# Two V rows per matmul, identity weights loaded once per twelve matmuls, and half of wd loaded in 16 pieces

## The chip, the cores and the metric

One core of one Trainium2 chip. The metric is the device time of one execution in microseconds (us). Runs agree within about 0.2%. Kernels are compared only within the same rounds.

## The reference, cut to what matters

```python
# B=4 sequences, one new token, D=640, 32 heads of Dh=192, 4096 cached positions, F=1536; bf16
h  = x + attention(layernorm(x) @ wq, k_cache, v_cache) @ wo
h2 = h + (silu(layernorm(h) @ w_gate) * (layernorm(h) @ w_up)) @ w_down
```

K and V are 201 MB each. Everything else is small: wq and wo 7.9 MB each, w_gate, w_up and w_down (wg, wu, wd below) 2.0 MB each. All of it is read once, 424 MB in all.

## The kernel before

K and V come in 128 loads of 3 MB (the last V in two halves) into a ring of six slots. A load is issued when its slot's last reader is done. For each of 64 steps (a pair of heads and a sequence), VectorE multiplies K by the query in two halves, TensorE sums groups of 16 products by an identity matmul, VectorE finishes the sums and the maximum, ScalarE takes the exponent, and TensorE multiplies the probabilities by V:

```python
def red(i, h):                      # 12 matmuls with the same weights, 128 times
    for j in range(J):              # J = 12
        matmul(psR[n % 3][:, 0:512], lhsT=identH, rhs=prod[n % NPR][:, :, j*16:(j+1)*16],
               start=(j == 0), stop=(j == J - 1))

def pv(i, lo=0, hi=T):              # 64 matmuls of 192 columns, 64 times
    for t in range(lo, hi):
        n = t % 4
        matmul(psO[p % 2][32*n:32*n + 8, 0:192], lhsT=pbuf[b][:, t, :], rhs=v[:, t, :], ...)

def o_t(p):                         # folds the four rows of psO, transposed; 16 times
    for j in range(3):
        for hh in range(2):
            matmul(psO[...], lhsT=orow[p % 2][:, j::3], rhs=r32[:, hh:8:2])
```

At the end wg, wu and wd are loaded into three slots of the ring, in that order, each by one transfer of 128 partitions; wd is waited for as a whole:

```python
wd_land = dma("sp", ... wdsb[:, :, :] <- wd viewed as "(q c) n -> q (c n)", c=12, [behind(n0 + 2)])
...
for c in range(12):
    for n in range(4):
        matmul(psH[32*n:32*n + 4, 0:160], lhsT=guT[:, c, 0:4], rhs=wdsb[:, c, n*160:(n+1)*160])  # waits: guT, wd_land
```

## Time and profile before

| | before |
|---|---|
| time, median of the first three runs | 1005.88 us |
| TensorE matmul busy, weight-load busy | 645.7, 296.7 us |
| TensorE instructions, matmuls and weight loads | 6736 + 6736 |
| load queue busy, share of 16 DMA engines | 98.9% |
| instruction packets (queue 8) | 53 |

The page of the kernel before: part 1 (busy time and share of each engine), the DMA row of part 2 (tenths busy in 40 slices), part 3 (queue: packets, MB, share of 16 engines) and the start of part 4 (the chain of waits by engine):

```profile
PE 645.7 (64%) x6736; PEld 296.7 (30%) x6736; DVE 547.5 (55%) x450; ACT 119.7 (12%) x412; POOL 4.5 (0%) x19
...
DMA  9999999999999999999999999999999999999995
...
q1 hardware_dynamic: 21472, 424.29, 98.9%
q8 instruction: 53, 0.87, 0.4%
...
DMA 68%; PE 21%; DVE 10%; SPq 1%; issue 0%; ACTq 0%; ACT 0%
```

No compute engine is near its limit, and the DMA engines are busy to the end. The line easily passed over is queue 8. Its 53 packets are 16 KB each (16384 bytes in the trace). Over TensorE's stream of 6736 + 6736 instructions that is 64.5 bytes and 254 instructions a packet, so I take them for the fetches of this stream.

The trace has 16 landing times for each of these loads, which I take for the shares of the 16 DMA engines of the page (by my count of the packet records, 16.1 packets are in flight on average between 100 and 900 us). This is my own listing of them for wd, the last load (us from the span's start):

```
988.47 988.71 988.81 988.91 989.19 990.08 991.86 993.05 | 998.10 998.36 998.43 999.02 999.31 999.55 999.75 999.92
```

Eight engines (below, the early eight) finish some 9 us ahead of the other eight (the late ones). The gap between the means of the two halves is 0.45 us for the first load of the run, 4.5 us at 504 us, and 9.0 us for wg. A load counts as landed only with its sixteenth part (wd's came at 999.92 us, and the wd matmuls that waited for it started at 1000.05), so the late eight set the pace.

The timeline of the last 16 us (start us, us taken, engine, line, operation, tiles; in brackets the engine's idle time before and what ended it), lnT being the normalized input of the second half and guT the input of the wd matmuls:

```profile
988.89 0.70 PE L398 MATMUL pb<-r,orow 128*64 128x4 f32 x12 [0.43 <-ACT orow L387]
...
993.25 0.35 DVE L256 STREAM_TRANSPOSE lnT<-lnrow 128x160 bf16<-128x160 bf16 x1
...
995.38 0.10 PEld L502 LDWEIGHTS pb<-wu_sb,lnT 128*4 128x4 bf16 x8 [0.67 <-DMA wu_sb<-in_B_w_up_dram]
...
997.87 0.85 DVE L508 STREAM_TRANSPOSE guT<-gu 128x384 bf16<-128x384 bf16 x1
...
1000.05 1.77 PE L512 MATMUL pb<-wd_sb,guT 128*4 128x160 bf16 x48 [2.90 <-DMA wd_sb<-in_B_w_down_dram]
```

guT is ready at 998.72 us, but the wd matmuls start at 1000.05, when wd's last part has landed (999.92).

### The profile page before, as it was taken

Reading aid. Unit: us, or ns where it says so; the run is one execution under the profiler, and the core shown is the slowest. Engines: PE = TensorE matmul, PEld = TensorE weight load, DVE = VectorE, ACT = ScalarE, POOL = GpSimd, SP = SyncE. Lnnn points to the kernel's source line nnn. Section 1 sums busy time; section 2 is a strip of 40 time slices with the busy share of each in tenths; the row PEclk is TensorE's granted clock in tenths of the full one; section 3 lists DMA queues with packets and bytes.
Section 4 is the critical chain, followed back from the end, with each engine's and each line's share of the span. In section 5 each row is a group of like instructions: output and inputs, shape, how many; then the busy total and the mean of one; then the engine's idle time right before and its main releaser. Section 6 shows DMA issues by size and latency. Waiting matters only on the chain.

```text
span 1004.3 us, 14803 instructions
## 1 busy us (share of the span) xinstructions
PE 645.7 (64%) x6736; PEld 296.7 (30%) x6736; DVE 547.5 (55%) x450; ACT 119.7 (12%) x412; POOL 4.5 (0%) x19
## 2 busy tenths in 40 slices
PE   0676666666576576576576676676676676576585
PEld 0232232333232232232232232232332332232243
DVE  2546546546546546546546546546546546546562
ACT  0111011011011011011010110110111010111012
POOL 1000000000000000000000000000000000000000
PEclk9787887887887888887887887887887877877887
DMA  9999999999999999999999999999999999999995
GB/s 394 426 435 430 426 431 427 428 431 427 429 429 427 429 429 431 428 427 431 427 430 428 430 426 431 425 433 430 425 431 429 428 429 428 431 428 429 428 425 248
DMA packets 21582, 425.24 MB, mean 423 GB/s; under 512 B 2448, under 2 KB 2448, under 8 KB 4496
## 3 DMA queue, kind: packets, MB, share of 16 engines
q1 hardware_dynamic: 21472, 424.29, 98.9%
q8 instruction: 53, 0.87, 0.4%
q14 instruction: 9, 0.07, 0.0%
q10 hardware_dynamic: 48, 0.01, 0.0%
HBM read 424.29 MB, written 0.01 MB: 422 GB/s over the span
## 4 chain that ended last, share of the span: by engine, by line
DMA 68%; PE 21%; DVE 10%; SPq 1%; issue 0%; ACTq 0%; ACT 0%
DMA ring<-in_A_k_cache_dram 64%; PE pb L319 15%; DVE prod L309 7%; PE pb L381 3%; DMA wd_sb<-in_B_w_down_dram 2%; DMA xrow<-in_A_x_dram 2%; DVE sc L325 1%; PE pb L334 1%; SPq L294 1%; PE pb L276 1%; DVE msb L330 0%; PE pb L344 0%; PE pb L365 0%; PE pb L398 0%; SPq L300 0%
## 5 line engine op out<-in xcount | busy, mean ns | idle before, releaser
L309 DVE TENSOR_TENSOR prod<-ring,qb 128x6144 f16<-128x6144 bf16 x128 | 429.2, 3354 | 308.3 <-DMA ring<-in_A_k_cache_dram 301.2
L319 PE MATMUL pb<-prod,identH 128*128 128x512 f16 x1536 | 470.6, 472 | 3.2 <-DVE prod L309 3.2
L319 PEld LDWEIGHTS pb<-prod,identH 128*128 128x128 f16 x1536 | 167.8, 116 | 262.1 <-issue 168.9
L334 PE MATMUL pb<-identF,msb 128*1 128x128 f32 x128 | 34.7, 369 | 320.5 <-DVE msb L330 320.5
L325 DVE TENSOR_REDUCE sc<-pb 128x32 f32<-128x512 f32 x128 | 88.0, 688 | 111.8 <-PE pb L319 111.8
L334 PEld LDWEIGHTS pb<-identF,msb 128*1 128x1 f32 x128 | 5.5, 80 | 335.9 <-DVE msb L330 335.9
L349 ACT ACTIVATE negM<-pb 128x1 f32<-128x1 f32 x64 | 11.0, 171 | 721.0 <-PE pb L344 721.0
L381 PE MATMUL pb<-ring,pbuf 128*8 128x192 bf16 x4096 | 95.8, 246 | 0.2 <-ACT pbuf L356 0.2
L381 PEld LDWEIGHTS pb<-ring,pbuf 128*8 128x8 bf16 x4096 | 81.3, 87 | 3.7 <-issue 0.4
L356 ACT ACTIVATE pbuf<-sc,negM 64x64 bf16<-64x64 f32 x128 | 73.7, 576 | 3.1
L356 ACT ACTIVATION_READ_ACCUMULATOR pbuf<-sc,negM 64x1 f32 x128 | 41.6, 325 | 0.0
L371 ACT ACTIVATE qb<-pb 128x192 bf16<-128x192 f32 x64 | 21.1, 330 | 102.5 <-PE pb L365 102.5
L344 PEld LDWEIGHTS pb<-negMc,ones_row 1*64 1x64 f32 x256 | 12.8, 136 | 35.0 <-issue 33.4
L344 PE MATMUL pb<-negMc,ones_row 1*64 1x1 f32 x256 | 18.3, 206 | 0.7 <-DVE negMc L338 0.7
L365 PE MATMUL pb<-qsb,sel 4*64 4x192 bf16 x128 | 17.2, 265 | 1.0 <-ACT qsb L280 0.6
L338 DVE TENSOR_REDUCE negMc<-pb 1x2 f32<-1x128 f32 x64 | 17.4, 271 | 0.5 <-PE pb L334 0.5
L246 PE MATMUL pb<-mv,quadm 128*128 128x2 f32 x4 | 1.0, 312 | 23.4 <-DVE mv L244 23.4
L330 DVE TENSOR_REDUCE msb<-sc 128x1 f32<-128x64 f32 x64 | 14.1, 220 | 2.2
L365 PEld LDWEIGHTS pb<-qsb,sel 4*64 4x64 bf16 x128 | 6.7, 101 | 27.9 <-issue 26.3
L398 PE MATMUL pb<-r,orow 128*64 128x4 f32 x192 | 11.1, 233 | 0.4 <-ACT orow L387 0.4
L398 PEld LDWEIGHTS pb<-r,orow 128*64 128x64 f32 x192 | 9.7, 173 | 2.1 <-ACT orow L387 0.7
L242 DVE BATCH_NORM_STATS2 stats<-xrow 128x6 f32<-128x160 bf16 x1 | 0.3, 328 | 16.2 <-DMA xrow<-in_A_x_dram 16.2
(60 smaller groups left out, 71.8 us busy)
## 6 DMA issues: line engine op xcount, KB each, us to landing
ring<-in_A_k_cache_dram SPq DMA_DIRECT2D x64, 3072.0 KB, 30.4
ring<-in_A_v_cache_dram SPq DMA_DIRECT2D x63, 3072.0 KB, 23.4
wq_sb<-in_A_wq_dram SPq DMA_DIRECT2D x1, 7680.0 KB, 21.2
wo<-in_A_wo_dram SPq DMA_DIRECT2D x16, 480.0 KB, 23.8
ring<-in_A_v_cache_dram SPq DMA_DIRECT2D x2, 1536.0 KB, 19.7
wg_sb<-in_B_w_gate_dram SPq DMA_DIRECT2D x1, 1920.0 KB, 26.2
wu_sb<-in_B_w_up_dram SPq DMA_DIRECT2D x1, 1920.0 KB, 19.4
wd_sb<-in_B_w_down_dram SPq DMA_DIRECT2D x1, 1920.0 KB, 23.6
```

The source lines that it names most:

```text
L309: tk["tt", n] = op("dve", lambda e: e.tensor_tensor(out=prod[n % NPR][:, :, :], in0=ring[slot[c]][:, h * TH:(h + 1) * TH, :], in1=qbs[i % ...
L319: tk["red", n] = op("pe", lambda e, j=j: e.matmul(psR[n % 3][:, 0:TH * R], lhsT=identH[:, :], rhs=prod[n % NPR][:, :, j * R:(j + 1) * R], ...
L325: tk["rsum", n] = op("dve", lambda e: e.tensor_reduce(sc[i % 3][:, h * TH:(h + 1) * TH], psR[n % 3][:, 0:TH * R].rearrange("q (t r) -> q t ...
L330: tk["rmax", i] = op("dve", lambda e: e.tensor_reduce(msb[i % 2][:, 0:1], sc[i % 3][:, :], AX.X, ALU.max), [g("rsum", 2 * i), g("rsum", 2 ...
L334: tk["maxT", i] = op("pe", lambda e: e.matmul(psS[0:1, 0:128], lhsT=msb[i % 2][:, 0:1], rhs=identF[:, :], start=True, stop=True), [g("rmax ...
L338: tk["hmax", i] = op("dve", lambda e: e.tensor_reduce(negMc[i % 2][0:1, 0:2], psS[0:1, 0:128].rearrange("o (h q) -> o h q", h=2), AX.X, AL ...
L344: tk["maxB", i] = op("pe", lambda e, hh=hh: e.matmul(psS[64 * hh:64 * hh + 64, 128:129], lhsT=ones_row[0:1, :], rhs=negMc[i % 2][0:1, hh:h ...
L356: tk["exp", i] = op("act", lambda e, hh=hh, r=r: e.activation(out=pbuf[b][r, :, 2 * b + hh], in_=sc[i % 3][r, :], func=ACTF.Exp, bias=negM ...
L365: tk["qb", i] = op("pe", lambda e, hh=hh: e.matmul(psQ[64 * hh:64 * hh + 64, 0:DH], lhsT=sel[32 * n:32 * n + B, b, :], rhs=qsb[32 * n:32 * ...
L371: tk["qbc", i] = op("act", lambda e: e.activation(out=qbs[i % 2][:, :], in_=psQ[:, 0:DH], func=ACTF.Copy, scale=QS), [g("qb", i), g("tt", ...
L381: tk["pv", i] = op("pe", lambda e, t=t, n=n: e.matmul(psO[p % 2][32 * n:32 * n + 2 * B, 0:DH], lhsT=pbuf[b][:, t, :], rhs=v[:, t, :], star ...
L398: tk["oT", p] = op("pe", lambda e, j=j, hh=hh: e.matmul(psO[p % 2][64 * hh:64 * hh + 64, 256 + 4 * j:260 + 4 * j], lhsT=orow[p % 2][:, j:: ...
```

## The change

Its intent: less work and fewer instructions on TensorE, and a better split of the last load over DMA engines. Two V rows go into one matmul (16 stationary columns, 384 moving columns; the two off-diagonal blocks are ignored). The identity weights stay in the array for eleven of twelve matmuls. The two matmuls that spread the maximum become one, and the fold `o_t` needs two accumulating matmuls in place of one. Half of wd (six of twelve rows of each partition) comes in 16 loads of 8 partitions, which are meant for the eight DMA engines that finish early. The other half comes in two loads over all 16.

```diff
+def held_matmul(e, out, lhsT, rhs, start, stop):
+    return e.add_instruction(mybir.InstMatmult(... ldweights=False, ...))
...
-            tk["red", n] = op("pe", lambda e, j=j: e.matmul(
+            tk["red", n] = op("pe", lambda e, j=j: (e.matmul if j == 0 else partial(held_matmul, e))(
...
-        for t in range(lo, hi):
-            n = t % 4
+        for t in range(lo, hi, 2):
+            n = (t // 2) % 4
...
-                psO[p % 2][32 * n:32 * n + 2 * B, 0:DH], lhsT=pbuf[b][:, t, :], rhs=v[:, t, :],
+                psO[p % 2][32 * n:32 * n + 4 * B, 0:2 * DH],
+                lhsT=pbuf[b][:, t:t + 2, :].rearrange("q t m -> q (t m)"),
+                rhs=v[:, t:t + 2, :].rearrange("q t d -> q (t d)"),
...
+                for k in range(2):          # o_t: twice the matmuls
...
-    wd_land = dma("sp", lambda e: e.dma_start(wdsb[:, :, :].rearrange("q c n -> q (c n)"),
-                                              wd[:, :].rearrange("(q c) n -> q (c n)", c=CF)),
-                  S_ring[(n0 + 2) % NS], [behind(n0 + 2)])
+    WDC = [(0, 6, sem("s_wd0")), (6, 10, sem("s_wd1")), (10, CF, sem("s_wd2"))]
+    wd_land = {}
+    for lo, hi, k in WDC:
+        nr = 8 if lo == 0 else 128
+        for r in range(0, 128, nr):
+            t = dma("sp", lambda e, lo=lo, hi=hi, r=r, nr=nr: e.dma_start(
+                wdsb[r:r + nr, lo:hi, :], wd[:, :].rearrange("(q c) n -> q c n", c=CF)[r:r + nr, lo:hi, :]),
+                k, [behind(n0 + 2)])
+        for c in range(lo, hi):
+            wd_land[c] = t
```

More of the change, by code (lines that the diff above doesn't have):

```diff
@@ L1 @@
 import math
+from functools import partial
 import concourse.bass as bass
@@ L91, in emit @@
         block.sync(run("sp"))
+def held_matmul(e, out, lhsT, rhs, start, stop):
+    return e.add_instruction(mybir.InstMatmult(
+        name=e.bass.get_next_instruction_name(), engine=mybir.EngineType.PE, start_tensor_calc=start,
+        stop_tensor_calc=stop, tile_size=(128, 128), tile_position=(0, 0), ldweights=False,
+        ins=[e.lower_ap(rhs), e.lower_ap(lhsT, for_matmul_weights=True)], outs=[e.lower_ap(out)]))
 class ExitGuard:
@@ L118, in build_kernel @@
     NS, NPR = 6, 3
+    OC = 2 * DH
     QS = 2.0 ** -4
@@ L145, in build_kernel @@
     r32 = sb("r32", [128, 32], FP32)
-    ones_row = sb("ones_row", [1, 64], FP32)
+    ones_row = sb("ones_row", [1, 128], FP32)
     epsv = sb("epsv", [128, 1], FP32)
@@ L155, in build_kernel @@
     negMc = [sb(f"negMc{j}", [1, 2], FP32) for j in range(2)]
-    negM = [sb(f"negM{j}", [128, 1], FP32) for j in range(2)]
+    negM = [sb(f"negM{j}", [128, 2], FP32) for j in range(2)]
     lsb = [sb(f"lsb{j}", [128, B], FP32) for j in range(2)]
     invL = sb("invL", [128, B], FP32)
-    orow = [sb(f"orow{j}", [128, DH], FP32) for j in range(2)]
+    orow = [sb(f"orow{j}", [128, 2 * DH], FP32) for j in range(2)]
     OT = [sb(f"OT{j}", [128, 3, B], BF16) for j in range(2)]
@@ L342, in max_b @@
     def max_b(i):
-        for hh in range(2):
-            tk["maxB", i] = op("pe", lambda e, hh=hh: e.matmul(
-                psS[64 * hh:64 * hh + 64, 128:129], lhsT=ones_row[0:1, :], rhs=negMc[i % 2][0:1, hh:hh + 1],
-                start=True, stop=True), [g("hmax", i), pool_done])
+        tk["maxB", i] = op("pe", lambda e: e.matmul(
+            psS[:, 128:130], lhsT=ones_row[0:1, :], rhs=negMc[i % 2][0:1, 0:2],
+            start=True, stop=True), [g("hmax", i), pool_done])
     def neg_m(i):
-        tk["negM", i] = op("act", lambda e: e.activation(out=negM[i % 2][:, :], in_=psS[:, 128:129], func=ACTF.Copy,
+        tk["negM", i] = op("act", lambda e: e.activation(out=negM[i % 2][:, :], in_=psS[:, 128:130], func=ACTF.Copy,
                                                          scale=alpha), [g("maxB", i)])
@@ L356, in exps @@
             tk["exp", i] = op("act", lambda e, hh=hh, r=r: e.activation(
-                out=pbuf[b][r, :, 2 * b + hh], in_=sc[i % 3][r, :], func=ACTF.Exp, bias=negM[i % 2][r, 0:1],
+                out=pbuf[b][r, :, 2 * b + hh], in_=sc[i % 3][r, :], func=ACTF.Exp, bias=negM[i % 2][r, hh:hh + 1],
                 scale=alpha, accum_out=lsb[p % 2][r, b:b + 1]),
@@ L377, in pv @@
         v = ring[slot[c]]
-        for t in range(lo, hi):
-            n = t % 4
+        for t in range(lo, hi, 2):
+            n = (t // 2) % 4
             land = landed[c][min(t // TH, len(landed[c]) - 1)]
             tk["pv", i] = op("pe", lambda e, t=t, n=n: e.matmul(
-                psO[p % 2][32 * n:32 * n + 2 * B, 0:DH], lhsT=pbuf[b][:, t, :], rhs=v[:, t, :],
-                start=(b == 0 and t < 4), stop=(b == B - 1 and t >= T - 4)), [land, g("exp", i), g("otc", p - 2)])
+                psO[p % 2][32 * n:32 * n + 4 * B, 0:2 * DH],
+                lhsT=pbuf[b][:, t:t + 2, :].rearrange("q t m -> q (t m)"),
+                rhs=v[:, t:t + 2, :].rearrange("q t d -> q (t d)"),
+                start=(b == 0 and t < 8), stop=(b == B - 1 and t >= T - 8)), [land, g("exp", i), g("otc", p - 2)])
         released[c] = tk["pv", i]
     def evac(p):
-        tk["evac", p] = op("act", lambda e: e.activation(out=orow[p % 2][:, :], in_=psO[p % 2][:, 0:DH],
+        tk["evac", p] = op("act", lambda e: e.activation(out=orow[p % 2][:, :], in_=psO[p % 2][:, 0:2 * DH],
                                                          func=ACTF.Copy), [g("pv", B * p + B - 1), g("oT", p - 2)])
@@ L397, in o_t @@
             for hh in range(2):
-                tk["oT", p] = op("pe", lambda e, j=j, hh=hh: e.matmul(
-                    psO[p % 2][64 * hh:64 * hh + 64, 256 + 4 * j:260 + 4 * j], lhsT=orow[p % 2][:, j::3],
-                    rhs=r32[:, hh:2 * B:2], start=True, stop=True), [g("evac", p), pool_done])
+                for k in range(2):
+                    tk["oT", p] = op("pe", lambda e, j=j, hh=hh, k=k: e.matmul(
+                        psO[p % 2][64 * hh:64 * hh + 64, OC + B * j:OC + B * (j + 1)],
+                        lhsT=orow[p % 2][:, k * DH + j:(k + 1) * DH:3],
+                        rhs=r32[:, 2 * B * k + hh:2 * B * (k + 1):2], start=(k == 0), stop=(k == 1)),
+                        [g("evac", p), pool_done])
     def inv_l(p):
@@ L406, in o_tc @@
         tk["otc", p] = op("dve", lambda e: e.tensor_tensor(
-            out=OT[p % 2][:, :, :], in0=psO[p % 2][:, 256:256 + 3 * B].rearrange("q (j b) -> q j b", b=B),
+            out=OT[p % 2][:, :, :], in0=psO[p % 2][:, OC:OC + 3 * B].rearrange("q (j b) -> q j b", b=B),
             in1=invL[:, None, :].broadcast_to([128, 3, B]), op=ALU.mult),
@@ L513, in build_kernel @@
                 psH[32 * n:32 * n + B, 0:DQ], lhsT=guT[:, c, 0:B], rhs=wdsb[:, c, n * DQ:(n + 1) * DQ],
-                start=False, stop=(c == CF - 1), skip_group_check=True), [gut, wd_land, ln2])
+                start=False, stop=(c == CF - 1), skip_group_check=True), [gut, wd_land[c], ln2])
     a = op("dve", lambda e: e.tensor_copy(out=outsb[:, :], in_=psH[:, 0:DQ]), [a])
```

## The prediction

> **What bounds it now.** The DMA engines. Page part 3: the load queue is busy 98.9% of 16 engines' span; slices read 9 throughout. TensorE (64%), VectorE (55%) and ScalarE (12%) are not limits; in the chain of waits the ring loads take 64%. Less TensorE work as such buys nothing before the last 30 us.
>
> **What is uneven.** The trace's landing records (16 increments a load, one an engine) split the engines into two groups of eight. For wd, eight land at 988.5 to 993.1 us, eight at 998.1 to 999.9. The gap of the group means grows evenly: 0.45 us at 22 us, 4.5 at 504, 9.2 at the end. Packets run back to back on both, so the late group does extra work: queue 8, "instruction", 53 packets of 16 KB. Their durations repeat with period eight, so I take them to go round eight engines. 53 x 256 = 13568 instructions, TensorE's stream (6736 + 6736). [...] Here a chunk with a fetch lands about 1.4 us late on one engine; 8.7 us x 8 / 53 gives 1.3 us a fetch. Every ring slot waits for the late group, which sets the pace.
>
> **What the change does.**
> 1. PV: 4096 to 2048 matmul and weight-load pairs. Reduction: 1536 weight loads to 128. maxB halves, oT doubles (192 to 384). TensorE's instructions fall from 13472 to about 8100: about 32 fetches, 21 fewer: 21 x 1.3 / 8 = 3.4 us earlier on the late group, hence in all landings; the gap at the end becomes about 5.7 us. This is the main gain; saved matmul time is hidden (at the low clock a reduction matmul takes 427 ns with or without a weight load).
> 2. wd: [...] At the measured 26.8 GB/s an engine (122.9 KB between the wu and wd landings, 4.58 us), the late group ends 2.3 us sooner and the early one 2.3 us later: both about 992 to 996. [...]
> 3. Tail (timeline): the compute from the last K landing to lnT at 993.6 moves with the loads (-3.4), plus oT 24 instead of 12 instructions (+0.6, from 0.70 us now) and a wider evacuation (+0.15). wu is then no longer the wait. guT ends near 996 instead of 998.7, and the wd matmuls start there instead of 1000.05, when wd landed; of the gain wd's landing allows 1.3 us.
>
> **Prediction.** 1005.9 - 3.4 (fetches) - 1.3 (wd) + 0.7 (oT, evacuation) gives 1001.9; [...] 1002.2 us, 8 in 10 within 1000.5 to 1004.6. Faster by over 2%: 0.01; within: 0.98; slower: 0.01.
>
> **What would show it.** Queue 8: about 32 packets. Gap of the landing groups before wd: 5 to 6 us. Busy PE and PEld down much, span down 0.4%. Half wd landed before guT ends. oT about 1.3 us at the tail.
>
> **What would make it wrong.** [...] Fetches whose cost doesn't follow their number. [...] half wd lands after 998. TensorE's clock staying low, so that its 14.6 us period is filled. The 16 extra issues (about 0.4 us each) coming too late.

The sum as it stands comes to 1001.9 us; the forecast is 1002.2. The 0.3 us between them stood for a possible loss through the 8-partition loads, which I guessed at 0 to 2 us; that term is cut, its ground not being shown. Cut too is the assumption that the half of wd in the 16 loads (0.98 MB) would go to the early eight engines; the 2.3 us each way and the 1.3 us for wd rest on it.

The figures of the prediction in the traces: 254 instructions a packet in the kernel before (the prediction counts 256). The packets of queue 8 take 1015 to 1107 ns, the first and last apart, in an order that repeats with every eighth (1072, 1068, 1059, 1099, 1099, 1087, 1018, 1018, then 1074, 1078, 1060, 1107, 1107, 1087, 1018, 1026). A packet of queue 8 began at 239.9 us; between the load whose last part landed at 240.85 us and the next, one landing of the sixteen slipped 1.5 us against the rest. From one reduction matmul's start to the next it is 427 ns (median) at a granted clock of 0.5 and 216 ns at 1.0, in the kernel before and in the changed one, where eleven of twelve have no weight load. One of the 64 steps takes 14.8 us (median). A load's issue took 0.33 or 0.43 us in the kernel before, and the 16 extra ones came 0.34 us apart.

## More of the kernel before

The stretches of the tail (us; busy time and instructions of each engine; then granted TensorE clock, DMA share, GB/s) show DMA share and throughput fall together, as engines finish:

```profile
984.00:989.00 5.00, 4.04 (x139) 3.10 (x140) 0.46 (x2) 3.15 (x8) 0.00 (x0) 1.00 0.94 397
989.00:994.00 5.00, 1.69 (x34) 1.13 (x38) 2.85 (x11) 1.58 (x2) 0.00 (x0) 0.80 0.58 243
```

## The result

1006.42 us, median of four runs (1006.26 to 1006.79), beside 1006.11 us before. The ratio is 1.0003, with a 95% interval of 0.9986 to 1.0021. Ratios here are the mean time of one kernel's runs over that of the other's of the same rounds, so not quite the ratio of the medians that I quote. The change gained nothing; 1002.2 us was forecast, 1000.5 at the least and 1004.6 at the most.

The page after: TensorE's weight loads and instructions and the queues are as forecast. Its matmul busy time is not: it rose from 645.7 to 658.7 us, where the prediction had "Busy PE and PEld down much". The V part raised it (662.2 us in pv_only, 647.5 in held_only, both below); how little such time counts, pad_time shows.

```profile
PE 658.7 (66%) x4752; PEld 121.5 (12%) x3344; DVE 547.6 (55%) x450; ACT 122.6 (12%) x412; POOL 4.5 (0%) x19
...
q1 hardware_dynamic: 21872, 424.29, 99.2%
q8 instruction: 32, 0.52, 0.2%
```

The timeline of the tail after, the same steps as before:

```profile
985.62 1.25 PE L412 MATMUL pb<-r,orow 128*64 128x4 f32 x24 [0.59 <-ACT orow L399]
...
990.73 0.35 DVE L266 STREAM_TRANSPOSE lnT<-lnrow 128x160 bf16<-128x160 bf16 x1
...
994.40 0.10 PEld L526 LDWEIGHTS pb<-wu_sb,lnT 128*4 128x4 bf16 x8 [2.21 <-DMA wu_sb<-in_B_w_up_dram]
...
996.89 0.85 DVE L532 STREAM_TRANSPOSE guT<-gu 128x384 bf16<-128x384 bf16 x1
...
999.39 0.97 PE L536 MATMUL pb<-wd_sb,guT 128*4 128x160 bf16 x24 [3.21 <-DMA wd_sb<-in_B_w_down_dram]
1000.79 1.22 PE L536 MATMUL pb<-wd_sb,guT 128*4 128x160 bf16 x24 [0.43 <-DMA wd_sb<-in_B_w_down_dram]
```

Read it from the top. The fold and lnT come 3.3 and 2.5 us earlier than before, although the fold takes 0.55 us longer: up to here the gain is there. Then TensorE waits 2.21 us for wu, where it had waited 0.67, and 3.21 us for the first half of wd. wu's last part lands at 994.36 us, 1.0 us before its old time although the loads ahead of it land over 3 us before theirs (wg: 987.44 in place of 990.78). wd's last part lands at 1001.53, 1.6 us after its old time.

The stretches of the tail after:

```profile
984.00:989.00 5.00, 3.01 (x56) 2.17 (x56) 1.69 (x7) 0.97 (x3) 0.00 (x0) 0.86 0.97 271
989.00:994.00 5.00, 2.00 (x22) 0.66 (x21) 1.34 (x5) 2.07 (x3) 0.00 (x0) 0.50 0.85 241
```

From 984 to 989 us the DMA share rose (0.94 to 0.97) and the throughput fell from 397 to 271 GB/s. The engines were as busy as before and moved less, so their packets took longer: by my count those of 15360 B that started in this stretch took 851 ns in the median, against 576 before.

So the theory after the result: the fetches were real and gave their gain, and the 8-partition loads took it back, because of the partitions of SBUF that they write while other loads still land. No trace shows by what way one load would hold up another, so the runs test only what can be measured: the same loads over neighbouring partitions or over partitions four apart (wd_step4), and on partitions 0 to 63 or 64 to 127 (wd_low, wd_high). Rivals: the fetches never mattered; the TensorE parts cost what wd gained; many small loads are slow by their size, their reads or their issue.

### The profile page after: what moved, and what is told of

Same layout as the page of the kernel before. It is cut to its first block, busy times and chain, and to the rows that moved or that the text cites. A ratio compares the mean times of both kernels' runs of the same rounds, so it can differ in the third digit from the quotient of the medians.

```text
span 1004.5 us, 9444 instructions
## 1 busy us (share of the span) xinstructions
PE 658.7 (66%) x4752; PEld 121.5 (12%) x3344; DVE 547.6 (55%) x450; ACT 122.6 (12%) x412; POOL 4.5 (0%) x19
## 3 DMA queue, kind: packets, MB, share of 16 engines
q1 hardware_dynamic: 21872, 424.29, 99.2%
## 4 chain that ended last, share of the span: by engine, by line
DMA 67%; PE 21%; DVE 10%; SPq 1%; issue 0%; ACTq 0%; ACT 0%
DMA ring<-in_A_k_cache_dram 63%; PE pb L97 13%; DVE prod L319 7%; PE pb L391 3%; DMA wd_sb<-in_B_w_down_dram 2%; DMA xrow<-in_A_x_dram 2%; PE pb L329 2%; DVE sc L335 1%; PE pb L344 1%; SPq L304 1%; PE pb L353 1%; PE pb L412 1%; PE pb L286 1%; DVE msb L340 1%; SPq L513 0%
## 5 line engine op out<-in xcount | busy, mean ns | idle before, releaser
L319 DVE TENSOR_TENSOR prod<-ring,qb 128x6144 f16<-128x6144 bf16 x128 | 429.1, 3353 | 305.6 <-DMA ring<-in_A_k_cache_dram 299.1
L97 PE MATMUL pb<-prod,identH 128*128 128x512 f16 x1408 | 432.3, 470 | 0.0
L358 ACT ACTIVATE negM<-pb 128x2 f32<-128x2 f32 x64 | 11.0, 172 | 715.6 <-PE pb L353 715.6
L391 PE MATMUL pb<-ring,pbuf 128*16 128x384 bf16 x2048 | 94.7, 326 | 0.2 <-ACT pbuf L365 0.2
L329 PE MATMUL pb<-prod,identH 128*128 128x512 f16 x128 | 61.2, 478 | 3.2 <-DVE prod L319 3.2
L353 PEld LDWEIGHTS pb<-negMc,ones_row 1*128 1x128 f32 x128 | 19.4, 189 | 279.4 <-issue 249.6
L391 PEld LDWEIGHTS pb<-ring,pbuf 128*16 128x16 bf16 x2048 | 46.3, 89 | 27.5 <-issue 0.5
L353 PE MATMUL pb<-negMc,ones_row 1*128 1x2 f32 x128 | 24.9, 262 | 0.7 <-DVE negMc L348 0.7
L412 PE MATMUL pb<-r,orow 128*64 128x4 f32 x384 | 20.0, 231 | 0.6 <-ACT orow L399 0.6
L412 PEld LDWEIGHTS pb<-r,orow 128*64 128x64 f32 x384 | 18.6, 174 | 2.4 <-ACT orow L399 1.0
L329 PEld LDWEIGHTS pb<-prod,identH 128*128 128x128 f16 x128 | 12.6, 99 | 32.1 <-issue 23.7
```

The source lines that it names most:

```text
L97: return e.add_instruction(mybir.InstMatmult(name=e.bass.get_next_instruction_name(), engine=mybir.EngineType.PE, start_tensor_calc=start, ...
L319: tk["tt", n] = op("dve", lambda e: e.tensor_tensor(out=prod[n % NPR][:, :, :], in0=ring[slot[c]][:, h * TH:(h + 1) * TH, :], in1=qbs[i % ...
L329: tk["red", n] = op("pe", lambda e, j=j: (e.matmul if j == 0 else partial(held_matmul, e))(psR[n % 3][:, 0:TH * R], lhsT=identH[:, :], rhs ...
L353: tk["maxB", i] = op("pe", lambda e: e.matmul(psS[:, 128:130], lhsT=ones_row[0:1, :], rhs=negMc[i % 2][0:1, 0:2], start=True, stop=True), ...
L391: tk["pv", i] = op("pe", lambda e, t=t, n=n: e.matmul(psO[p % 2][32 * n:32 * n + 4 * B, 0:2 * DH], lhsT=pbuf[b][:, t:t + 2, :].rearrange(" ...
L412: tk["oT", p] = op("pe", lambda e, j=j, hh=hh, k=k: e.matmul(psO[p % 2][64 * hh:64 * hh + 64, OC + B * j:OC + B * (j + 1)], lhsT=orow[p % ...
```

## The experiments

All but two gave correct results. Packet times below are my own count from the trace's packet records: "7680 B" are the packets of the 16 loads, "15360 B" those of wg, wu (and of an undivided wd), which take 573 to 592 ns undisturbed.

### undo_wd: the change without its wd part

```diff
-    WDC = ...; 16 loads of 8 partitions and 2 of 128
+    wd_land = dma("sp", ... one load of 128 partitions, as before)
```

> The changed kernel with wd loaded again by one transfer of 128 partitions. Theory (fetches are DMA work of the late eight engines[...]): 32 packets on queue 8, gap of the two landing groups 5.2 to 5.8 us at the end, wu lands near 992, wd near 996.5, time 1002.4 us (1001.8 to 1003.2). Rival (instruction fetches cost nothing that is waited for, and the wd part is neutral): 1006.2 us as before.

Measured: 1001.87 us, ratio 0.9952 (0.994 to 0.9965), 32 instruction packets, gap of the landing groups 4.8 us at wg, wu landed at 991.00 and wd at 995.56. The stretch and the step that waited in this run:

```profile
984.00:989.00 5.00, 2.01 (x38) 1.63 (x38) 2.44 (x10) 1.03 (x3) 0.00 (x0) 0.96 0.97 406
...
995.70 1.77 PE L528 MATMUL pb<-wd_sb,guT 128*4 128x160 bf16 x48 [2.83 <-DMA wd_sb<-in_B_w_down_dram]
```

What follows: the TensorE parts gain 4.8 us (0.0048 x 1006), and the wd part takes all of it back. The rival that the TensorE parts cost what wd gained is out. That it is the fetches through which these parts gain is not shown yet; pad43 and pad_time are for that.

### only_wd: the kernel before with the new wd loads alone

```diff
-    wd_land = dma("sp", ... one load of 128 partitions)
+    WDC = ...; 16 loads of 8 partitions and 2 of 128, as in the change
```

> The kernel before with the new wd loads alone. Theory [...]: 53 packets on queue 8; the 7680-byte packets take a median well over their shortest; the wu landing moves later than 995.3 us by 1 to 3 us, wd is complete at 1001 to 1004 us, time 1007 to 1010 us. Rival (the rebalancing of engines works as meant, the loss of the whole change comes from the TensorE parts): wd complete by 998, time 1004.6 us.

Measured: 1010.75 us, ratio 1.0042 (1.0029 to 1.0056). wu landed at 1000.07 (995.34 before), wd at 1005.96. The 7680 B packets took 428 ns in the median and up to 624; their shortest took 291. The stretch:

```profile
984.00:989.00 5.00, 3.99 (x136) 3.05 (x136) 0.68 (x3) 2.98 (x8) 0.00 (x0) 1.00 0.94 255
```

The loss is in the wd loads alone, 4.2 us here. wu came even later than I expected (4.7 us, not 1 to 3), and so did wd and the end.

### wd_step4: the 16 loads over partitions four apart

```diff
-        for r in range(0, 128, nr):          # partitions r .. r+7
+        rows = [slice(32*j + s, 32*j + s + 29, 4) for j in range(4) for s in range(4)]   # 8 partitions, 4 apart
```

> The changed kernel with the same 16 loads of 8 partitions, but of partitions 4 apart[...]. Theory [...]: the first eight loads (partitions 0 to 63) have packets of 291 to 310 ns; those of partitions 64 to 127 [...] are slower; time 1002.5 to 1004.5 us. Rival (the cost is that of many small loads: their number, their size of 7680 bytes, their issue): packets as before (median 398 ns, up to 567) and time 1006.4 us.

Measured: 1006.34 us, ratio 0.9998 (0.9986 to 1.0011). The time missed the expectation; the packets met it. The first 32 packets of 7680 B, those that began before 986.4 us, took 291 to 301 ns; then, as the loads of partitions 64 to 127 began, they rose, to a median of 566 ns between 986.6 and 994 us. Of the 82 packets of 15360 B that started after 984.5 us, 49 took more than 800 ns, up to 1349. Both about doubled, and this hits wu, which TensorE waits for next.

Neighbouring partitions cost something too. In the change itself the first packet of 7680 B began at 983.58 us, so if an engine takes its loads in order, none was at its ninth load (partition 64) before 985.9 (eight packets of 291 ns). Yet the 21 packets of 15360 B that began there from 984.3 to 985.9 took 738 to 1052 ns, against 573 to 581 in wd_step4, which differs only in the partitions of each load. From 985 to 986 us some ten packets of 15360 B were in flight at a time (10.2 on average) and four of 7680 B (3.9). Four writers were there beside ten others, and all ten were slow. How the slowness gets to the others stays open.

Whether the bytes of partitions 64 to 127 or merely the later loads are slow, this run can't tell; wd_low and wd_high can.

### wd_low and wd_high: the same loads, written to one half of the partitions

```diff
+    wdx = spare room behind wd in the same ring slot
+            if nr == 8 and (rs.start < 64) != True:       # wd_high: != False
+                dst, ds = wdx, slice(rs.start - 64, rs.stop - 64, 4)   # wd_high: + 64
```

The sources, sizes, engines and issues are those of wd_step4. The wd matmuls of that half use 64 partitions.

> wd_step4 with the second eight loads writing their bytes to spare room on partitions 0 to 63 in place of 64 to 127; same sources, sizes, engines and issue. The result is wrong on purpose (the first half of wd is used on 64 partitions alone). Theory [...]: the 7680-byte packets take 291 to 310 ns throughout, the late engines' 15360-byte packets of wu 573 to 590 ns, wu lands near 991, wd is complete near 995.5 us, time 1001.5 us (1000.8 to 1002.8). Rival (small loads, their reads from memory or their issue are slow): as wd_step4, 1006.3 us.

Measured: 1002.64 us, ratio 0.9962 (0.9948 to 0.9976). All 128 packets of 7680 B took 291 to 298 ns, and those of 15360 B 573 to 592, but for one of 1065. wu landed at 991.18, wd at 997.78, later than the 995.5 I expected.

> The opposite of wd_low: all 16 loads write to partitions 64 to 127 (wrong result on purpose). Theory: 7680-byte packets at 560 ns or more from the start while late engines still load, the late engines' wu packets near 1000 to 1150 ns from 984 us on, wu lands after 995, time 1008 us or more (1007 to 1013). Rival: as wd_step4, 1006.3 us.

Measured: 1010.37 us, ratio 1.0039 (1.0026 to 1.0053). The 7680 B packets took 565 ns in the median, wu's packets 1126, and wu landed at 997.11. The stretches of wd_step4:

```profile
984.00:989.00 5.00, 3.20 (x56) 2.23 (x56) 1.69 (x7) 0.92 (x3) 0.00 (x0) 0.78 1.01 301
```

of wd_low:

```profile
984.00:989.00 5.00, 3.20 (x59) 2.22 (x56) 1.69 (x7) 1.11 (x3) 0.00 (x0) 0.82 0.97 387
```

and of wd_high:

```profile
984.00:989.00 5.00, 2.87 (x55) 1.95 (x55) 1.79 (x8) 0.81 (x3) 0.00 (x0) 1.00 1.04 237
```

Only the destination differs between the three, and with it how many partitions the matmuls of that half use: 387, 301 and 237 GB/s with none, half and all of the loads on partitions 64 to 127, and 1002.64, 1006.34 and 1010.37 us. The rival of slow small loads falls: in wd_low they take 291 to 298 ns, where 291 is the shortest in the change itself. What counts is which partitions they write while other loads are still landing.

Yet wd_low is no faster than undo_wd, and its wd landed 2.2 us later. Its landings tell why. Each of the 16 loads has eight landings with its data, so eight engines carry them, 16 packets each. Six engines had landed wu by 985.5 us. But from 986 to 987 us only four packets of 7680 B were in flight, and two engines landed their share of wd's second piece at 987.93 and 988.24. Had they carried 16 packets of 291 ns after wu (984.26 at the earliest), and then the 1.6 us of that piece (an estimate: eight packets of 196 ns, the shortest of this size in the changed kernel's trace; 102 ns for the third piece), they would have landed it at 990.5. So at least two of the early eight carried none of the 16 loads, and at least two of the late ones did. The last two shares of wd fit: two late engines landed wu at 990.45 and 990.77; 4.7 us for the 16 packets and 1.6 and 0.8 us for the two other pieces give 997.5 and 997.8, and they landed at 997.45 and 997.78. The half of wd did not go where the time was free. Besides, fewer fetches had already cut the gap of 9.0 us to 4.8, and moving half of wd changes it by about 4.6 (an estimate, twice the 2.3 us of the prediction), so there was little left to balance.

### wd_chunks: three pieces, each over all 16 engines

```diff
-        nr = 8 if lo == 0 else 128
+        nr = 128
```

> The changed kernel with wd in its three pieces, each one load of 128 partitions over 16 engines. Theory: as undo_wd, with the first wd matmuls not later; 1002.0 us (1001.4 to 1003.0), and no 7680-byte packet slowed beyond some 300 ns. Rival (splitting wd into pieces is what costs): 1005 to 1006.5 us.

Measured: 1001.54 us, ratio 0.9949 (0.9935 to 0.9963). Its 7680 B packets took 291 to 302 ns; wu landed at 991.10 and the last of wd at 995.76. The stretch, and the wd matmuls, which no longer wait for wd:

```profile
984.00:989.00 5.00, 3.01 (x56) 2.17 (x56) 1.69 (x7) 0.97 (x3) 0.00 (x0) 0.93 0.97 400
...
996.11 1.00 PE L536 MATMUL pb<-wd_sb,guT 128*4 128x160 bf16 x48 [1.61 <-DVE guT L532]
```

This beats both kernels, by 0.5%. It is not told apart from undo_wd (0.9949 and 0.9952, with intervals that overlap). undo_wd's wait for wd is gone, but guT ended 1.6 us later in this profile (996.05 against 994.43 us), so whether cutting wd in pieces gains anything stays open.

### pad43 and pad_time: instructions back without work, and work without instructions

```diff
             pv(i - 2)
+            for _ in range(43):                       # pad43: 86 instructions a step
+                matmul(psS[0:1, 400:401], lhsT=identB[:, 0:1], rhs=identB[:, 0:1])
+            for d in range(12):                       # pad_time instead: 13 instructions a step
+                (matmul if d == 0 else held_matmul)(psS[:, 260:500], lhsT=identB, rhs=identB, 240 columns)
```

Both start from undo_wd.

> undo_wd with 43 useless one-column matmuls (86 instructions) per batch in 62 of the 64 steps: TensorE's instruction count is that of the kernel before again, with no new load and nothing waiting for them. Theory (instruction fetches delay the late engines): 53 packets on queue 8, gap of the landing groups near 9 us again, time 1005.3 us (1004.6 to 1006.2), 3.4 us over undo_wd. Rival (the gain of undo_wd comes from fewer or quicker TensorE operations, not from fetches): gap 5.4 us, time within 0.5 us of 1001.9.

> Control for pad43: undo_wd with TensorE time added in few instructions, one weight load and 12 matmuls of 240 columns (13 instructions) per step. Theory (fetches): about 35 packets on queue 8, gap below 6.3 us, time 1002.4 us (1001.7 to 1003.2). Rival (TensorE time is what counts): as slow as pad43 or slower, over 1004.5 us.

Measured: pad43 1007.22 us, ratio 1.001 (0.9998 to 1.0023); pad_time 1003.09 us, ratio 0.9969 (0.9956 to 0.9983). Busy times and queue 8 of pad43:

```profile
PE 728.9 (73%) x7418; PEld 195.8 (19%) x6010; DVE 547.7 (54%) x450; ACT 122.5 (12%) x412; POOL 4.5 (0%) x19
...
q8 instruction: 52, 0.85, 0.3%
```

and of pad_time:

```profile
PE 729.6 (73%) x5496; PEld 127.9 (13%) x3406; DVE 547.4 (55%) x450; ACT 122.6 (12%) x412; POOL 4.5 (0%) x19
...
q8 instruction: 35, 0.57, 0.2%
```

The two add the same matmul time, 68 us. With the instructions the gap at wg is 8.9 us again and wg lands at 991.07; with the time alone the gap is 5.5 and wg lands at 987.90. The fetches cause the gap; TensorE's time does not. pad43 is 1.9 us slower than the 1005.3 that I expected, 1.0 over the range. Both run the padding in the last step of the loop too, where TensorE's 1.1 us (68 over 62 steps) is on the chain; that would account for a part of it, though I did not test it apart. In pad43 the wd matmuls wait for guT (1001.84 us), not for wd (1000.22), so the landings are the cleaner measure here.

### held_only and pv_only: the two TensorE parts apart

```diff
 held_only: the kernel before, with held_matmul for j > 0 in red()
 pv_only:   undo_wd, with e.matmul for every j in red()
```

> The kernel before with the held identity weights alone: 1408 weight loads fewer. Theory: 47 or 48 packets on queue 8, gap near 8.2 us, 0.9 us under before (ratio 0.999). Rival (one weight load in place of twelve shortens the reductions on a chain that counts): more than 2 us.

> undo_wd without the held weights, so the two V rows per matmul alone (with the merged maxB and doubled oT): 37 or 38 packets on queue 8, gap near 6.3 us, 1002.8 us (1002.2 to 1003.6) by the theory of fetches, most of the gain of undo_wd. Rival (the held weights bring the gain): near 1006.

Measured: held_only 1004.41 us, ratio 0.9984 (0.9972 to 0.9997), 47 packets; pv_only 1003.23 us, ratio 0.9973 (0.9961 to 0.9986), 37 packets. That is 1.6 and 2.7 us, together 4.3 of undo_wd's 4.8. held_only's gain is somewhat over the 0.9 expected, and its interval holds that too.

Put side by side, one profile each, the landing of wg follows the number of fetches, whatever made it:

| kernel | instruction packets | gap at wg, us | wg landed, us |
|---|---|---|---|
| before | 53 | 9.0 | 990.78 |
| pad43 | 52 | 8.9 | 991.07 |
| held_only | 47 | 7.8 | 989.63 |
| pv_only | 37 | 6.3 | 988.25 |
| pad_time | 35 | 5.5 | 987.90 |
| undo_wd | 32 | 4.8 | 986.44 |

From the first row to the last: (990.78 - 986.44) / 21 is 0.21 us of the kernel's pace for each fetch, or 1.65 us on the one engine of eight that does it. The bytes alone would take it 0.61 us at the 26.8 GB/s that an engine moves (15360 B in 573 ns).

## Why the prediction was wrong

- **What bounds the kernel: right.** DMA is busy to the end (load queue 98.9% before, 99.2% after, 98.8 to 99.3% in the experiments whose queues I asked for), and VectorE's wait for K is some 300 us before and after (301.2 and 299.1).
- **Step 1, the fetches: right in mechanism, the size somewhat low.** 32 packets were forecast and found. I took 1.3 us a fetch on its engine, which gave 3.4 us; the landings of wg came 4.3 us earlier in undo_wd. pad43 and pad_time show that it is the instruction count.
- **Step 2, wd: this is the step that failed.** "the late group ends 2.3 us sooner and the early one 2.3 us later", with a possible loss that I put at 0 to 2 us, was wrong in two ways. First, the loss. The estimate took it for a small matter of the 16 loads themselves. In fact these slowed the packets of some ten engines beside them, wu's among them, from 573 to 738 ns and more within a microsecond of their start, and to about double in wd_step4 once they wrote partitions 64 to 127. The loss vanished when all bytes went to partitions 0 to 63, four apart (wd_low), and doubled when all went to the other half (wd_high): ratios 0.9962, 0.9998 (wd_step4, half and half) and 1.0039. Second, the assumption that the early eight would carry the loads: at least two of the eight engines that carried the loads were late ones (wd_low's landings). The term that I put at a gain of 1.3 us less a loss of 0 to 2 us measured as a loss: the ratio goes from 0.9952 (undo_wd) to 1.0003, 5.1 us, and it is 4.2 us in only_wd. The destination alone is worth 3.6 us (wd_low to wd_step4); what the wrong engines add, up to 1 us (undo_wd to wd_low), lies within the intervals.
- **Step 3, the tail: right until it met wu.** lnT "at 993.6 moves with the loads (-3.4), plus oT 24 instead of 12 instructions (+0.6, from 0.70 us now) and a wider evacuation (+0.15)" gives 991.0; it ended at 991.08. "wu is then no longer the wait" was nearly true of undo_wd (0.5 us of waiting) and false of the change (2.2 us), because the wd loads slowed wu.
- **The listed risk** "half wd lands after 998" is what happened: the last of that half landed at 999.25. I named it and gave it too little weight. The page had no line for it.

Still open: what passes the slowness on to engines that carried none of the 16 loads at the time; and what neighbouring partitions would cost on partitions 0 to 63 alone, for which there is no run. That the fetches go round the late eight engines is inferred from the gap's growth with their number, since the trace doesn't name an engine.

## What to carry to other kernels

When the DMA engines are the limit, look at the packets of the instruction queue too: here cutting TensorE's instruction count by 5400 took 21 of 53 of them away and gained 0.5%, where TensorE's time was not the limit. When loads are to be moved from one DMA engine to another, ask which SBUF partitions they write while other loads land: here the same 16 loads cost nothing that was measured, 3.6 us or 7.7 us by their destination alone. And find out from the landings which engines are free; two or more of the eight were not. And when a change has several parts and the sum is zero, undo one part first: here a single run showed a gain and a loss of the same size.
